# Two-layer attention and MLP kernel: Vector score tiles pick a head on an idle row tile, and the planner's settings are replaced

## The chip, the cores and the metric

The kernel runs on one core of one Trainium2 chip. The metric is device time in microseconds (us) of one execution; lower is better. The engines are TensorE (PE), VectorE (DVE), ScalarE (ACT), GpSimd (POOL) and SyncE (SP, which issues the DMAs).

## The reference

The input is x with 2048 tokens of width 512. Two rounds, each of an attention and an MLP with residuals, use the same weights. The attention has 32 heads of width 16 and no mask, so each head has a full 2048 x 2048 score matrix.

```python
def A(x, wqkv, wo):                     # H = 32, Dh = 16
    q, k, v = heads(x @ wqkv)
    p = softmax(q @ k.T * Dh ** -0.5)
    return merge(p @ v) @ wo
def B(x, w1, b1, w2, b2):               # F = 1376
    return gelu(layernorm(x) @ w1 + b1) @ w2 + b2
x = x + A(layernorm(x)); x = x + B(layernorm(x))
x = x + A(layernorm(x)); x = x + B(layernorm(x))
```

## The kernel before

**The tiling.** Layers are numbered 1 and 3 for the two attentions. Attention work is cut into segments: a chunk of queries (512 tokens; the last chunk of layer 3 is cut in two of 256) times a group of four heads. A segment has 64 score tiles of 128 keys x 512 queries (in the last two chunks one tile holds two key blocks of 256 queries), 4096 over the whole program. The four heads of a group lie on partitions 0, 32, 64 and 96, so that the score matmul of head `hp` uses the 32-row tile `hp` of TensorE's array; four such row tiles can hold four matmuls at once. The tiles of a segment are listed key block by key block, and in a block head by head.

**Two ways to the exponential.** Most score tiles go to ScalarE: `flow_scores` takes two or three tiles at a time in turn (after an opening with two at a time), puts them into PSUM banks 0 to 2 or 3 to 4, and one ACTIVATE (line 1414) writes exp of the whole group to `PT`. The tiles of every third key block (`DK` = 3, 6, 9, 12, 15) may go to VectorE instead ("d" tiles, list `todod` of the segment). Such a tile is put in bank 5 (`DLANE`) or bank 7 (`MISCB`); `d_load` (line 1512) adds a constant and writes 16-bit integers that are the bits of an approximate exp, and `job_d` (line 1545) makes three shifted copies of two tiles at a time. The four versions are multiplied with four scaled versions of the values (`V`, `vs`). A d tile that VectorE has not taken by the time the other tiles are used up goes to ScalarE.

**Values.** `try_pv` collects ready tiles and issues the value matmuls (line 1615) on the four 32-column tiles of the array, one column tile for each head, into bank 6; a d tile needs four of them, a ScalarE tile one. When a segment is complete its sums are transposed (line 1645), divided and stored. The linear layers (lines 941, 1694, 1749, 1792) run on the full array beside all this. [...]

**The order.** No engine's order is written by hand. At build time a planner (`Sched`) keeps a clock for each engine with a cost for each operation, always starts the task that can start first, and fixes the five instruction orders. They run on the chip in that order, with semaphores where one engine needs another's result. After planning, `refill` puts matmuls on zeros (`zw`, lines 1321, 1323, 1325) into TensorE's planned gaps.

A d tile is chosen by `take_d`, in three places: with a group of ScalarE tiles (`flow_scores`, which passes the heads of that group), after a VectorE task or a load of a d tile when VectorE has little to do (`d_solo`), and in a long gap of TensorE (`fill_pe`). The head is chosen by one line, and `d_solo` and `fill_pe` pass an empty list of heads:

```python
        j = next((j for j in sg["todod"] if sg["tiles"][j][1] not in hps), sg["todod"][0])
```

**The settings.** `Hint` holds six settings of the planner: how little work VectorE must have for `d_solo` (`D_IDLE`), how full a group of value matmuls must be (`PV_LEAST`), how long other TensorE work may delay the next scores (`HOLD_LATE`), how near in time a ready tile must be (`PV_NEAR`), the priority of the second half of a linear matmul (`LIN2`), and whether a tile of a ScalarE group may be given to VectorE (`D_STEAL`). There are ten modes: the base, and nine that change one setting. Every 8 groups `flow_scores` calls `HINT.at`, which reads the next mode from the string `ORDER`.

Of the kernel before, what the change touches and what calls it, by code (L numbers as in the profile page):

```python
# [506 lines left out]

class Hint:
    BASE = dict(D_IDLE=1.2, PV_LEAST=0.75, HOLD_LATE=0.4, PV_NEAR=0.7, LIN2=9, D_STEAL=0)
    MODES = ({}, dict(D_IDLE=0.8), dict(D_IDLE=1.7), dict(PV_LEAST=0.6), dict(PV_LEAST=0.9), dict(HOLD_LATE=0.2), dict(HOLD_LATE=0.6), dict(PV_NEAR=0.4), dict(LIN2=0.9), dict(D_STEAL=1.0))  # L510
    STEP = 8
    ORDER = '0550000002700000070000000900000050000000000400000000000000000000040000000050000070000000300000004000300050000090000000000070040010000000007002040000050804080004'

    def mode(self, k):
        self.__dict__.update(self.BASE)
        self.__dict__.update(self.MODES[k])

    def at(self, step):
        self.mode(int(self.ORDER[step]) if step < len(self.ORDER) else 0)


HINT = Hint()
# [3 lines left out]
class Builder:  # L526
# [806 lines left out]
    def flow_scores(self):  # L1333

        S_, P = self.S_, self.P
        self.cur = 0
        gi = 0
        self.batch = None
        self.ptuse = {}
        self.lane_busy = False  # L1340
        self.lanes = {}
        self.nsteal = 0
        self.dload = 0
        for b in range(4):
            S_.retire("mb", b, ("ret", b))
        last = {}
        while True:
            if gi % Hint.STEP == 0:
                HINT.at(gi // Hint.STEP)
            self.advance()  # L1350
            if self.cur == len(self.segs):
                break
            sg = self.segs[self.cur]
            if not self.wide and not (sg["L"] == 1 and sg["nparts"] == 2 and sg["part"] == 0):
                self.wide = True
                gi += gi % 2
                for b in (4, 5):
                    S_.retire("mb", b, ("ret", b))
            if self.wide:
                b0, G = ((0, 3), (3, 2))[gi % 2]  # L1360
            else:
                b0, G = ((0, 2), (2, 2))[gi % 2]
            grp = []
            while len(grp) < G:
                self.advance()
                if self.cur == len(self.segs):
                    break
                sg = self.segs[self.cur]
                grp.append((sg, (sg["todo"] or sg["todod"]).pop(0)))
            for sg, j in grp:  # L1370
                if sg["nt"] - self.left(sg) >= GELU_FROM * sg["nt"]:
                    S_.mark(("under", sg["i"]))
            banks = list(range(b0, b0 + len(grp)))
            keys = [("ret", b) for b in banks] + [("free", last[b]) for b in banks if b in last]
            for sg, j in grp:
                keys += [("qt", sg["i"])] + self.kv_keys(sg, sg["tiles"][j][0])
            yield ("keys", keys)
            for b in banks:
                last[b] = gi
            ptn = "pt3" if gi % 2 == 0 else "pt2"  # L1380
            self.starved = not S_.pools[ptn].free
            if self.starved:
                self.try_pv()
            pt = yield ("get", ptn)
            self.starved = False
            yield ("ready", "pe", (), [("ps", b) for b in banks])
            dts = []
            while self.wide and len(grp) + len(dts) < 4:
                d = self.take_d([s_["tiles"][j][1] for s_, j in grp] + [s_["tiles"][j][1] for s_, j, b, bt, w in dts])
                if d is None:  # L1390
                    break
                dts.append(d)
            if self.wide and not dts and len(grp) in (3,) and self.dve_work() < HINT.D_STEAL:
                d = self.take_d([s_["tiles"][j][1] for s_, j in grp[:-1]], banks[-1])
                if d is not None:
                    sg, j = grp.pop()
                    (sg["todod"] if set(sg["tiles"][j][0]) <= set(DK) else sg["todo"]).insert(0, j)
                    last[banks.pop()] = ("lane", gi)
                    self.lanes[d[2]] = ("lane", gi)
                    self.cur = min(self.cur, sg["i"])  # L1400
                    self.nsteal += 1
                    dts.append(d)
            ops = []
            for (sg, j), b in zip(grp, banks):
                ops.append(self.score(sg, j, b))
            for d in dts:
                S_.submit(Task("pe", -0.5, self.score(d[0], d[1], d[2])), cb=lambda d=d: self.d_load(d))
            if len(ops[0]) > 1:
                ops = [[o[i] for o in ops] for i in range(len(ops[0]))]
            ops = [o for part in ops for o in part]  # L1410
            yield Task("pe", 0.0, ops)
            n = len(grp)
            self.ptuse[(ptn, pt)] = n
            S_.submit(Task("act", 1e-5 * gi, [I(lambda e, pt=pt, n=n, b0=b0: e.activation(out=self.PT[:, pt:pt + n, :], in_=self.ps[:, b0:b0 + n, :], func=ACTF.Exp, scale=EXPS),  # L1414
                                                [("ps", b) for b in banks], [("pt", pt + k) for k in range(n)], 0.19 + 0.4275 * n)]),
                      cb=lambda grp=grp, pt=pt, gi=gi, ptn=ptn: (S_.mark(("free", gi)), self.p_ready([(sg, j, ("pt", pt + k), self.PT[:, pt + k, :], (ptn, pt), 0) for k, (sg, j) in enumerate(grp)])))
            if self.batch is not None and not dts and self.cur < len(self.segs) and self.left(self.segs[self.cur]) < DTAIL and self.batch["tiles"][0][0] is self.segs[self.cur]:
                self.close_batch()
            gi += 1
        yield ("keys", [("free", g) for g in set(last.values())])  # L1420
        for b in range(6):
            S_.release("mb", b)
        S_.mark(("scores_done",))
# [19 lines left out]
    def take_d(self, hps, lane=None):  # L1443

        S_, P = self.S_, self.P
        self.advance()
        if self.cur == len(self.segs) or self.dload > 1 or P.free["dve"] - S_.now > 1.3 or sum(o[4] for t in S_.pend["dve"] for o in t.ops) > DBACK:
            return None
        if self.batch is None and (not S_.pools["dp"].free or S_.pools["dp"].waiters or self.flying >= DFLY):
            return None  # L1450
        mb = S_.pools["mb"]
        soon = lambda b: P.ready("pe", (), [("ps", b)]) <= max(S_.now, P.free["pe"]) + 0.1
        if lane is not None:
            b = lane
        elif not self.lane_busy and ("ret", DLANE) in S_.done and soon(DLANE):
            b = DLANE
        elif MISCB in mb.free and not mb.waiters and soon(MISCB):
            b = MISCB
        else:
            return None  # L1460
        sg = self.segs[self.cur]
        if self.left(sg) < DTAIL:
            if self.cur + 1 == len(self.segs):
                return None
            sg = self.segs[self.cur + 1]
            if sg["nt"] - self.left(sg) >= (DAHEAD if ("retq", 5) in S_.done else DAHEAD // 2):
                return None
        if not sg["todod"]:
            return None
        j = next((j for j in sg["todod"] if sg["tiles"][j][1] not in hps), sg["todod"][0])  # L1470
        kbs = sg["tiles"][j][0]
        if not all(k in self.S_.done for k in [("qt", sg["i"])] + self.kv_keys(sg, kbs) + [("vs", sg["i"], kb) for kb in kbs]):
            return None
        if b == DLANE:
            self.lane_busy = True
        elif lane is None:
            mb.free.remove(b)
        self.dload += 1
        sg["todod"].remove(j)
        sg["n"] += len(SHIFT) - 1  # L1480
        bt = self.batch
        if bt is None:
            bt = self.batch = {"unit": S_.pools["dp"].free.pop(0), "tiles": [], "loaded": 0, "closed": False}
            self.ptuse[("dp", bt["unit"])] = 1
            self.flying += 1
        w = len(bt["tiles"])
        bt["tiles"].append((sg, j))
        if w + 1 == DBATCH:
            self.batch = None
        return (sg, j, b, bt, w)  # L1490

    def d_solo(self):

        S_ = self.S_
        if not self.wide or self.dve_work() > HINT.D_IDLE:
            return
        d = self.take_d([])
        if d is not None:
            S_.submit(Task("pe", D_PRIO, self.score(d[0], d[1], d[2])), cb=lambda: self.d_load(d))

# [474 lines left out]
```

## Time and profile before

| what | value |
|---|---|
| median of 3 runs | 1582.37 us (1582.03 to 1583.13) |
| the profiled execution | 1583.48 us, of which the span is 1581.7 us |
| PE busy | 1549.1 us, 98% of the span |
| ACT busy | 1524.5 us, 96% |
| DVE busy | 1450.7 us, 92% |
| POOL busy | 332.3 us, 21% |
| exps on ACT (line 1414) | 1279 instructions, 1445.8 us |
| loads of d tiles on DVE (line 1512) | 946 instructions, 631.8 us |
| shifted copies on DVE (line 1545) | 1440 instructions, 558.2 us |

The table is from the page of one profiled execution. The span is the time from its first to its last instruction; the execution's own time holds 1.8 us more. Busy time is the time in which an engine ran at least one instruction, so overlapping instructions are counted once; a mean duration times a count can therefore be more than the busy time. PE's busy time contains the matmuls on zeros. In lines about groups, the part after the first bar is busy time and mean nanoseconds of one instruction, the part after the second bar is the idle time just before such instructions and what ended most of it.

### The profile page before, as it was taken

To read this page: it belongs to the slowest core of one execution; us is meant where nothing else is said; L and a number is where in the kernel's file an instruction comes from. 1 tells how busy PE (TensorE), PEld (TensorE's weight loads), DVE (VectorE), ACT (ScalarE), POOL (GpSimd) and SP (SyncE) were. 2 spreads that over 40 slices of the span, in tenths; PEclk is the share of its full clock that TensorE was granted. 3 is DMA by queue.
4 is the path that set the end of the run, shared out by engine and by line. 5 is a ranking of instruction groups with operands and counts; after the bars stand their busy time and mean duration, and the time that the engine had idled before them with its cause. 6 is when DMAs were issued, how large, how long until landed. Compare 5 with 4: busy or idle time off the path is not lost.

```text
span 1581.7 us, 38782 instructions
## 1 busy us (share of the span) xinstructions
PE 1549.1 (98%) x16223; PEld 471.7 (30%) x16223; DVE 1450.7 (92%) x3210; ACT 1524.5 (96%) x1362; POOL 332.3 (21%) x574
## 2 busy tenths in 40 slices
PE   9999999999999999999999999999999999999998
PEld 3222222222222222222222223222222222344454
DVE  7689999999999899989999898999999999999894
ACT  6999999999999999999999999999999999999996
POOL 5586321001210022202212227320001000020100
PEclk9999999999999999999999999999999999999999
DMA  6663112103321133213742223210001100221200
GB/s 173 114 143 88 32 31 44 48 24 70 85 45 47 28 75 76 55 38 99 133 62 56 61 71 76 54 33 22 24 22 38 32 23 18 40 41 35 50 19 21
DMA packets 212463, 88.77 MB, mean 56 GB/s; under 512 B 183835, under 2 KB 206656, under 8 KB 212288
## 3 DMA queue, kind: packets, MB, share of 16 engines
q1 hardware_dynamic: 212288, 86.29, 24.4%
q8 instruction: 127, 2.08, 0.6%
q14 instruction: 48, 0.39, 0.1%
HBM read 34.65 MB, written 19.48 MB: 34 GB/s over the span
## 4 chain that ended last, share of the span: by engine, by line
PE 54%; DVE 23%; ACT 20%; issue 2%; POOL 0%; SPq 0%; DMA 0%; POOLq 0%; DVEq 0%
ACT PT L1414 19%; PE ps L1429 19%; PE ps L1615 16%; DVE dp L1512 10%; DVE dp L1545 7%; PE ps L1749 5%; PE ps L1792 4%; PE ps L941 4%; PE ps L1321 3%; PE ps L1694 1%; DVE accT L1645 1%; PE ps L1325 1%; PE ps L1323 1%; ACT h L1784 1%; DVE n L1006 1%
## 5 line engine op out<-in xcount | busy, mean ns | idle before, releaser
L1414 ACT ACTIVATE PT<-ps 128x1536 bf16<-128x1536 f32 (+1 forms) x1279 | 1445.8, 1259 | 30.2 <-PE ps L1429 24.2
L1512 DVE TENSOR_SCALAR dp<-ps 128x512 uint16<-128x512 f32 x946 | 631.8, 679 | 60.4 <-PE ps L1429 57.9
L1429 PE MATMUL ps<-QT,KT 32*128 32x512 bf16 (+1 forms) x4608 | 672.3, 358 | 13.9 <-DVE dp L1512 5.2
L1545 DVE TENSOR_SCALAR dp<-dp 128x1024 uint16<-128x1024 uint16 x1440 | 558.2, 427 | 6.1 <-PE ps L1615 1.7
L1615 PE MATMUL ps<-PT,V 128*17 128x512 bf16 (+1 forms) x3540 | 468.9, 358 | 0.1
L1615 PE MATMUL ps<-dp,vs 128*17 128x512 bf16 (+1 forms) x3204 | 438.5, 357 | 0.9 <-DVE dp L1545 0.9
L1429 PEld LDWEIGHTS ps<-QT,KT 32*128 32x128 bf16 x4608 | 172.1, 91 | 546.6 <-ACT PT L1414 258.5
L1158 POOL TENSOR_SCALAR QT<-qraw,scl,qbias 128x512 bf16<-128x512 bf16 (+1 forms) x84 | 71.6, 853 | 807.6 <-PE ps L1429 803.2
L1615 PE MATMUL ps<-dp,V 128*17 128x512 bf16 (+1 forms) x1068 | 212.5, 357 | 2.7 <-DVE accT L1645 2.1
L1323 PE MATMUL ps<-zw 32*128 32x444 bf16 (+4 forms) x697 | 189.2, 322 | 0.0
L1615 PEld LDWEIGHTS ps<-dp,vs 128*17 128x17 bf16 x3204 | 111.4, 88 | 118.8 <-issue 97.0
L1615 PEld LDWEIGHTS ps<-PT,V 128*17 128x17 bf16 x3540 | 112.9, 88 | 112.6 <-issue 99.4
L1321 PE MATMUL ps<-zw 128*128 128x448 bf16 (+13 forms) x475 | 113.7, 335 | 2.9 <-DVE ps L741 1.7
L1325 PE MATMUL ps<-zw 128*32 128x448 bf16 (+24 forms) x1202 | 111.7, 320 | 0.3 <-DVE dp L1512 0.2
L1749 PE MATMUL ps<-yT,wf 128*128 128x512 bf16 (+3 forms) x396 | 101.7, 360 | 1.6 <-DVE accT L1645 0.8
L941 PE MATMUL ps<-wqkv,xnT 128*128 128x512 bf16 x336 | 95.3, 383 | 1.6 <-DVE qy L1013 0.4
L1183 POOL TENSOR_SCALAR vs<-V 128x340 bf16<-128x340 bf16 (+2 forms) x72 | 60.5, 842 | 30.3 <-PE ps L1615 23.1
L1615 PEld LDWEIGHTS ps<-dp,V 128*17 128x17 bf16 x1068 | 52.4, 88 | 43.9 <-issue 23.1
L1645 DVE STREAM_TRANSPOSE accT<-ps 128x512 f32<-128x512 f32 (+1 forms) x88 | 57.7, 656 | 8.0 <-PE ps L1615 6.7
L1773 DVE TENSOR_SCALAR h<-ps,b1c 128x512 bf16<-128x512 f32 (+2 forms) x88 | 62.0, 705 | 3.2 <-PE ps L1749 2.9
L1321 PEld LDWEIGHTS ps<-zw 128*128 128x128 bf16 x475 | 37.2, 99 | 72.7 <-issue 44.0
L882 POOL TENSOR_SCALAR xn<-xres,rs,nmr 128x512 bf16<-128x512 bf16 x54 | 53.4, 996 | 10.6 <-DMA xnT<-xn 5.1
(179 smaller groups left out, 888.4 us busy)
## 6 DMA issues: line engine op xcount, KB each, us to landing
vs<-vs_scr SPq DMA_DIRECT2D x56, 255.0 KB, 2.7
wf<-in_B_w_dram SPq DMA_DIRECT2D x90, 128.0 KB, 2.5
q_scr<-qk SPq DMA_DIRECT2D x22, 256.0 KB, 2.1
k_scr<-qk SPq DMA_DIRECT2D x12, 256.0 KB, 2.0
out_dram<-xres SPq DMA_DIRECT2D x16, 128.0 KB, 1.7
vs_scr<-vs SPq DMA_DIRECT2D x8, 255.0 KB, 3.5
xres<-in_A_x_dram SPq DMA_DIRECT2D x7, 256.0 KB, 3.2
v_scr<-vst SPq DMA_DIRECT2D x12, 136.0 KB, 2.0
```

Of the source, the lines that this page charges most:

```text
L941: yield Task("pe", prio if c0 == 0 else min(prio, HINT.LIN2), [I(lambda e, c=c: e.matmul(self.ps[:, b, :], lhsT=xnT[:, c, :], rhs=self.wqk ...
L1158: yield Task(eng, 0.4, [I(lambda e: e.tensor_scalar(out=self.QT[:, q, 0:W], in0=src, scalar1=self.scl[:, k, hg:hg + 1], scalar2=self.qbias ...
L1321: fn = lambda e: e.matmul(self.ps[:, b, 0:w], lhsT=self.zw[:, 0:128], rhs=self.zw[:, 0:w], start=st, stop=st, skip_group_check=True)
L1323: fn = lambda e: e.matmul(self.ps[:, b, 0:w], lhsT=self.zw[32 * p:32 * p + 32, 0:128], rhs=self.zw[32 * p:32 * p + 32, 0:w], start=st, sto ...
L1325: fn = lambda e: e.matmul(self.ps[32 * p:32 * p + 32, b, 0:w], lhsT=self.zw[:, 0:32], rhs=self.zw[:, 0:w], start=st, stop=st, skip_group_c ...
L1414: S_.submit(Task("act", 1e-5 * gi, [I(lambda e, pt=pt, n=n, b0=b0: e.activation(out=self.PT[:, pt:pt + n, :], in_=self.ps[:, b0:b0 + n, :] ...
L1429: return [I(lambda e, kb=kb, i=i: e.matmul(self.ps[:, b, i * W:(i + 1) * W], lhsT=self.KT[32 * hp:32 * hp + 32, hg, kb * 128:(kb + 1) * 12 ...
L1512: self.S_.submit(Task("dve", 0.0, [I(lambda e: e.tensor_scalar(out=self.dp[:, u, w * 512:(w + 1) * 512], in0=self.ps[:, b, :], scalar1=BIT ...
L1545: yield Task("dve", pr, [I(lambda e, k=k, v=v: e.tensor_scalar(out=self.dp[:, v, 0:N], in0=self.dp[:, u, 0:N], scalar1=float(SHIFT[k]), sc ...
L1615: ops.append((nth[j, sh] + 0.1 * i, I(lambda e, hp=hp, v=v, ap=ap[:, i * W:(i + 1) * W], first=first and i == 0, W=W: e.matmul(self.ps[32 ...
L1645: yield Task("dve", 0.3, [I(lambda e: e.transpose(self.accT[:, a, 0:W], self.ps[:, ACCB, 0:W]), [("ps", ACCB)], [RA], 0.17 + 0.535 * W / 5 ...
L1749: yield Task("pe", pr if c0 == 0 else min(pr, HINT.LIN2), [I(lambda e, c=c: e.matmul(self.ps[0:M, b, off:off + W], lhsT=self.w1(fc, c), rh ...
```

## The change

Three things are changed.

1. `take_d` looks at TensorE before it picks the head of a d tile. It works out the time `t` at which the tile could start, collects the heads whose row tile is still busy then (only if TensorE is in row mode), and picks the first d tile whose head is not busy; among those, one whose head is not in the list `hps` it was given.
2. `flow_scores` remembers the heads of the group that it is about to issue in `self.group` until the group has been issued, and `d_solo` passes this list where it passed an empty one.
3. The string `ORDER` is new: 159 digits where there were 160, with 104 that are not the base mode where there were 27. The first digits differ as well, from the second on. The ten modes are the same; digits are read in base 36, which makes no difference for 0 to 9.

```diff
-    ORDER = '0550000002700000070000000900000050000000000400000000000000000000040000000050000070000000300000004000300050000090000000000070040010000000007002040000050804080004'
+    ORDER = '005555003180310019413073040330407885455803010030028129180000730440110100040007002434339950550723032320234308400953830012333075908409591072300003698000049440985'
...
     def at(self, step):
-        self.mode(int(self.ORDER[step]) if step < len(self.ORDER) else 0)
+        self.mode(int(self.ORDER[step], 36) if step < len(self.ORDER) else 0)
...
         self.batch = None
+        self.group = []
         self.ptuse = {}
...
+            self.group = [s_["tiles"][j][1] for s_, j in grp]
             yield ("keys", keys)
...
             yield Task("pe", 0.0, ops)
+            self.group = []
             n = len(grp)
...
-        j = next((j for j in sg["todod"] if sg["tiles"][j][1] not in hps), sg["todod"][0])
+        t = max(P.free["pe"], S_.now, P.ready("pe", (), [("ps", b)]))
+        busy = [hp for hp, x in P.tiles.items() if x > t + 0.02] if P.tiling == "row" else []
+        j = min(sg["todod"], key=lambda j: (sg["tiles"][j][1] in busy, sg["tiles"][j][1] in hps))
...
-        d = self.take_d([])
+        d = self.take_d(self.group)
```

`P.tiles` is the planner's record of when each row tile becomes free, and `P.free["pe"]` of when TensorE can issue again. As the planner makes the whole order anew, instructions move on every engine.

More of the change, by code (lines that the diff above doesn't have):

```diff
@@ L509 @@
     BASE = dict(D_IDLE=1.2, PV_LEAST=0.75, HOLD_LATE=0.4, PV_NEAR=0.7, LIN2=9, D_STEAL=0)
-    MODES = ({}, dict(D_IDLE=0.8), dict(D_IDLE=1.7), dict(PV_LEAST=0.6), dict(PV_LEAST=0.9), dict(HOLD_LATE=0.2), dict(HOLD_LATE=0.6), dict(PV_NEAR=0.4), dict(LIN2=0.9), dict(D_STEAL=1.0))
+    MODES = (dict(), dict(D_IDLE=0.8), dict(D_IDLE=1.7), dict(PV_LEAST=0.6), dict(PV_LEAST=0.9), dict(HOLD_LATE=0.2), dict(HOLD_LATE=0.6), dict(PV_NEAR=0.4), dict(LIN2=0.9), dict(D_STEAL=1.0))
     STEP = 8
-    ORDER = '0550000002700000070000000900000050000000000400000000000000000000040000000050000070000000300000004000300050000090000000000070040010000000007002040000050804080004'
+    ORDER = '005555003180310019413073040330407885455803010030028129180000730440110100040007002434339950550723032320234308400953830012333075908409591072300003698000049440985'
     def mode(self, k):
```

## The prediction

> **What bounds the kernel now.** I read the page's first part, then busy time by stretch, then what ScalarE (ACT) waits for, then the groups kept apart by shape, then stretches of the timeline. The page (engine, busy us, share, instructions):
>
> ```profile
> PE 1549.1 (98%) x16223; PEld 471.7 (30%) x16223; DVE 1450.7 (92%) x3210; ACT 1524.5 (96%) x1362; POOL 332.3 (21%) x574
> ```
>
> Three engines look full. PE's 98% holds matmuls on zeros (lines 1321, 1323, 1325), so it is not the measure. The stretches (columns: busy us of PE, weight load, DVE, ACT, POOL; clock; DMA) show more:
>
> ```profile
> 40.00:1560.00 1520.00, 1494.79 (x15882) 447.55 (x15885) 1414.17 (x3111) 1490.58 (x1312) 308.01 (x507) 1.00 0.24 54
> 640.00:960.00 320.00, 314.00 (x2938) 88.20 (x2930) 297.52 (x648) 305.93 (x262) 71.70 (x124) 1.00 0.35 75
> 120.00:1480.00 1360.00, 1338.14 (x13938) 389.15 (x13930) 1288.30 (x2840) 1335.49 (x1168) 251.21 (x421) 1.00 0.23 51
> ```
>
> From 40 to 1560 us ACT idles 1520 - 1490.6 = 29.4 us, 14.1 of them between 640 and 960 us, where layer 1's end meets layer 3's start. In the long middle (120 to 1480 us) DVE idles 1360 - 1288.3 = 71.7 us. So ACT is the bound; what it waits for between 40 and 1560 us, and between 640 and 960 us (us in total, times, longest):
>
> ```profile
> ACT PT L1414 <- PE ps L1429: 21.6, 61, 1.7
> ACT dw L1665 <- DVE dw L1664: 1.3, 4, 0.4
> ```
> ```profile
> ACT PT L1414 <- PE ps L1429: 12.6, 23, 1.7
> ```
>
> It waits for scores from PE, hardly for DVE. The groups by shape give the prices:
>
> ```profile
> L1414 ACT ACTIVATE PT<-ps 128x1536 bf16<-128x1536 f32 x593 | 882.1, 1487 | 14.9 <-PE ps L1429 9.6
> L1414 ACT ACTIVATE PT<-ps 128x1024 bf16<-128x1024 f32 x685 | 718.0, 1063 | 15.3 <-PE ps L1429 14.6
> L1512 DVE TENSOR_SCALAR dp<-ps 128x512 uint16<-128x512 f32 x946 | 631.8, 679 | 60.4 <-PE ps L1429 57.9
> L1545 DVE TENSOR_SCALAR dp<-dp 128x1024 uint16<-128x1024 uint16 x1398 | 548.4, 431 | 6.1 <-PE ps L1615 1.7
> L1545 DVE TENSOR_SCALAR dp<-dp 128x512 uint16<-128x512 uint16 x42 | 11.0, 293 | 0.1
> ```
>
> One 512-column score tile costs ACT 1487 - 1063 = 424 ns. Exps overlap, so the instruction's own cost comes from the page's 1445.8 us for all 1279 of them: (1445.8 - 3150 x 0.424) / 1279 = 0.086 us, with 4096 - 946 = 3150 tiles on ACT. A stretch without a wait agrees within 1%: 34 exps in 38.69 us against 34 x (2.5 x 0.424 + 0.086) = 39.0.
>
> ```profile
> 1126.65 38.69 ACT L1414 ACTIVATE PT<-ps 128x1536 bf16<-128x1536 f32 x34
> ```
>
> The timeline of PE tells what a row tile is worth (start, length from the first start to the last end):
>
> ```profile
> 1153.49 0.60 PE L1429 MATMUL ps<-QT,KT 32*128 32x512 bf16 x4
> 1154.03 0.60 PE L1792 MATMUL ps<-wqkv,h 128*128 128x512 bf16 x2
> 1154.56 0.39 PE L1429 MATMUL ps<-QT,KT 32*128 32x512 bf16 x2
> 1154.88 0.60 PE L1792 MATMUL ps<-wqkv,h 128*128 128x512 bf16 x2
> ```
> ```profile
> 25.19 0.40 PE L1429 MATMUL ps<-QT,KT 32*128 32x512 bf16 x4
> 25.52 1.25 PE L1321 MATMUL ps<-zw 128*128 128x448 bf16 x6
> ```
>
> Four scores on four heads hold PE 25.52 - 25.19 = 0.33 us; four of which two share a head hold it 0.54. Two scores side by side: 0.32. So a matmul behind another on one row tile costs 0.21 us, one on an idle row tile nothing, and 0.32 - 0.21 = 0.11 us goes with the change of tiling mode.
>
> **What the Trainium skill says.** "TensorEngine Tiling (Array Packing)", Key Properties: a change of tiling mode drains TensorE, and tiles work in parallel. The trace agrees, with 0.11 us for the change and 0.33 against 0.54 for four scores. "ScalarE: Activation LUTs", What ACT_TABLE_LOAD costs: 186 ns + 0.833 ns per column, and some 93 ns of overlap back to back. That is 427 ns a tile and 93 ns an instruction; the trace has 424 and 86, which I use. "TensorE: Matmul & The Clock Gate", part 1: the array's clock falls after too little work in a window of about 3.4 us. The clock column above is 1.00 throughout; no fall shows.
>
> **The change, part by part.** The planner is in the kernel, so built instruction orders can be compared; all counts below are from there.
>
> *ACT.* Vector tiles rise from 946 to 964, so ACT's fall from 3150 to 3132, in 1271 instructions instead of 1279 (three fewer of 1536 columns, four of 1024, the one of 512). 18 x 0.424 + 8 x 0.086 = **8.3 us** less. All of it lies on the bounding engine. The gelus and their tables stay, as do the first 100 or so ACT instructions, and so the opening.
>
> *PE, scores.* Without the zero matmuls, I cut PE's stream into runs of one tiling mode and took in each run the fullest tile. Over all score runs that is 380.6 us at 2400 columns a us, and 313.8 after: **66.8 us** less. Runs two scores deep fall from 509 to 231, one deep rise from 562 to 885. This is what choosing the head does.
>
> *PE, given back.* The value matmuls' fullest tiles rise from 402.6 to 418.8 us (+16.2): 63 more matmuls for 18 more shifted tiles (3 x 21), and heads less even. Mode changes 2431 to 2458: 27 x 0.11 = +3.0. Net PE need: 1045.0 + 267 = 1312 before; 994.4 + 270 = 1265 after, **47.6 us** less. It is not time gained; it is worth what it takes from ACT's 21.6 us of waits.
>
> *How much of those.* I cut both orders into 40 parts of equal score work and set PE's need (0.115 us a change) against ACT's (tiles x 0.459). Leaving out the first and last parts, PE needs more than ACT in seven parts before, by 25.3 us in all, near the 21.6 measured. After, it does in three, by 8.2: at the join of the layers 11.7 becomes 7.3, elsewhere 13.6 becomes 0.9. Taken whole, two thirds of the waits would go, 15 us. But 12.6 of the waits lie at the join, where the relief is 38% (4.7 us). Of the 9.0 elsewhere, 3.4 come before 120 us, where little changes, and the rest are waits of mostly 0.2 to 0.4 us, about the length of a score run, which less work need not remove: I count a quarter (1.4). So I take **6 us**; ends: 15 gained, and 6 lost if the dense new order waits in other places.
>
> *DVE.* 18 loads x 0.668 (631.8/946) = 12.0; 39 more shifts of 1024 x 0.392 = 15.3; 24 fewer of 512 x 0.26 = -6.3: 21 us more. It is covered by the 71.7 us of idle in the middle, which shrinks to about 42 as the stretch shortens by 8. Costed at nothing; if the cover is gone it shows as PE waiting for banks 5 and 7.
>
> *Zero matmuls.* 2374 to 2838: 759 more on column tiles, 244 fewer on row tiles, 51 fewer full. They stand in PE's planned gaps. Work weighted by tile size, zeros included, goes from 1005 to 1021 us, so the clock has no reason to fall. Cost: nothing; bounds 0 to +3 us if they hold up scores.
>
> *POOL and SP.* 578 and 524 instructions in both, some rearranged: query transposes (1144) and loads of vs (1174) pass the xnT transposes (918). POOL waits 803 us on PE for QT, that is, it works far ahead; these moves cost nothing while that lead holds. For DMA I find at most 2 us waits in the trace: bounds -1 to +2.
>
> Sum against the profiled execution: span 1581.7 - 8.3 - 6 = 1567.4; that execution took 1583.48 (1.8 around the span), so 1569.2. The median of the runs shown is 1582.37, 1.1 below it: **1568 us**.
>
> **The rivals.**
> *PE was the whole limit of the waits.* Two thirds or more of ACT's waits vanish, as the cut in 40 parts says word for word: 1582.4 - 8.3 - 15 = 1559, and down to 1554. For it: PE holds 54% of the chain that ended last. Against: the join of the layers keeps its dense linear work. Chance 0.15.
> *The relief goes nowhere.* Freed PE time is filled with zeros and ACT's waits stay or grow by up to 6: 1574 to 1580. For it: the trace has ACT 98% busy in the middle already, so there is little to win. Chance 0.20, a fifth of it within 0.2%.
> *DVE becomes the bound: slower.* With about 42 us of slack in 1350, a late load (1512) keeps bank 5 or 7; PE runs in order, so the next score of a Vector tile waits, the ACT scores behind it wait, and ACT idles. PE already waits 58.4 us for 1512 in 154 places. It decides from the point where new ACT idle passes 8.3 us; if ACT's waits double with it (+22), 1582.4 - 8.3 + 22 = 1596. Against: of all these waits just 21.6 us reach ACT now. Chance 0.08.
> *It doesn't do what it says.* Excluded for the order (depth falls), not for the chip: four row tiles could run slower than two. The 0.33 us for four speaks against it; it would end within 0.2% (0.02).
>
> **How the numbers follow.** Forecast (1562 to 1574): 0.55; rivals 0.15, 0.20, 0.08, 0.02. A measurement of this kernel tells about 0.2% (3.2 us) from no change. Faster: 0.55 + 0.15 + 0.16 = 0.86; same: 0.04 + 0.02 = 0.06; slower 0.08. The range 1556 to 1579 holds the forecast, most of the first rival and most of the second.
>
> **What would show it.** ACT busy near 1516; 964 loads at 0.68; score groups in runs of 0.39 rather than 0.60; less DVE idle before 1512; ACT's waits on PE under 21.6, the fall outside 640 to 960 us larger. Wrong if ACT's idle between 40 us and its last exp grows past 37 us, if waits name DVE, or if the clock column drops.

## The result and the profile after

The changed kernel takes 1565.56 us (median; 1563.94 to 1566.4 in 4 runs), the kernel before 1582.75 us in the runs beside it. The ratio is 0.9887 (95% interval 0.987 to 0.9904), so it is 17.2 us faster; 14.4 were predicted. Its profiled execution took 1565.7 us with a span of 1563.9 us. The mean granted clock was 0.999 in all four runs; of the 39 runs of the kernel before that stand beside e11, those at 0.999 took 1.9 us longer (median) than those at 1.000. Lines behind the added ones stand up to 5 lower: 1414 is now 1417, 1429 is 1432, 1512 is 1517, 1545 is 1550, 1615 is 1620.

The page's first part:

```profile
PE 1519.7 (97%) x16750; PEld 486.1 (31%) x16750; DVE 1458.7 (93%) x3243; ACT 1510.3 (97%) x1354; POOL 328.9 (21%) x574
```

The span is 17.8 us shorter and ACT is busy 14.2 us less. The busy time of the engines by stretch (the ends moved with the span), and what ACT waits for from 40 us to its last exp, then between 640 and 960 us:

```profile
40.00:1545.00 1505.00, 1468.35 (x16446) 463.26 (x16439) 1424.81 (x3153) 1478.47 (x1306) 304.56 (x508) 1.00 0.25 54
640.00:960.00 320.00, 310.74 (x3060) 91.86 (x3062) 297.76 (x648) 309.19 (x267) 76.40 (x134) 1.00 0.36 75
120.00:1470.00 1350.00, 1317.17 (x14530) 406.35 (x14534) 1299.16 (x2876) 1331.84 (x1169) 244.14 (x416) 1.00 0.23 51
```
```profile
ACT PT L1417 <- PE ps L1432: 19.7, 39, 3.4
```
```profile
ACT PT L1417 <- PE ps L1432: 9.2, 13, 2.4
```

The waits are 39 instead of 61, but their sum falls by only 1.9 us, and only at the join of the layers (12.6 to 9.2). DVE's idle in the middle falls from 71.7 to 50.8 us. The groups by shape:

```profile
L1417 ACT ACTIVATE PT<-ps 128x1536 bf16<-128x1536 f32 x590 | 890.5, 1509 | 14.9 <-PE ps L1432 12.2
L1417 ACT ACTIVATE PT<-ps 128x1024 bf16<-128x1024 f32 x681 | 726.9, 1081 | 10.8 <-PE ps L1432 10.2
L1517 DVE TENSOR_SCALAR dp<-ps 128x512 uint16<-128x512 f32 x964 | 641.8, 679 | 27.1 <-PE ps L1432 24.1
L1550 DVE TENSOR_SCALAR dp<-dp 128x1024 uint16<-128x1024 uint16 x1437 | 561.2, 430 | 4.4 <-PE ps L1620 2.2
L1550 DVE TENSOR_SCALAR dp<-dp 128x512 uint16<-128x512 uint16 x18 | 4.6, 286 | 0.0
```

An exp's mean duration rose by 20 ns, and yet ACT is busy for less. An instruction that waits in ACT's queue behind a running exp starts before that one ends, and the overlap is counted in both. A longer mean here means more exps that were ready in time: of those with 1536 columns, 377 had all their scores 0.2 us or more before the running exp ended, and 441 have after the change. With less lead the recorded duration is 1.45 us, with more it is up to 1.53 us (medians), at the same time from end to end. DVE's idle before a load of a d tile (line 1517) halved, from 60.4 to 27.1 us.

All score matmuls, before and after:

```profile
L1429 PE MATMUL ps<-QT,KT 32*128 32x512 bf16 (+1 forms) x4608 | 672.3, 358 | 13.9 <-DVE dp L1512 5.2
```
```profile
L1432 PE MATMUL ps<-QT,KT 32*128 32x512 bf16 (+1 forms) x4608 | 600.8, 359 | 22.0 <-ACT PT L1417 9.1
```

The same 4608 matmuls keep PE busy for 71.5 us less. Four scores in a row, whose length says that each has its own row tile:

```profile
1119.77 0.39 PE L1432 MATMUL ps<-QT,KT 32*128 32x512 bf16 x4
1120.09 0.38 PE L1620 MATMUL ps<-dp,vs 128*17 128x512 bf16 x1
```

Four scores hold PE for 1120.09 - 1119.77 = 0.32 us, much as four on different heads did in the opening of the kernel before (0.33). And the longest pieces of the chain that ended last (start, us, what), first before, then after:

```profile
1145.14 53.24 ACT PT L1414 x47
```
```profile
1118.08 99.54 ACT PT L1417 x88
1299.73 96.50 ACT PT L1417 x85
```

In that chain ACT now runs up to 88 exps in a row without anything holding it up, where it was 47. Of the whole chain ACT now holds 44% and PE 31%; before, PE held 54% and ACT 20%.

**Where the 17 us come from.** Waits miss a part of what a late exp costs, so I took the time from the end of one exp to the end of the next. Where the second was queued well ahead, the median is 1.343 us for 1536 columns and 0.916 for 1024, in both kernels: 0.427 us a tile and 0.062 an instruction. (The Trainium skill has 0.833 ns a column in "ScalarE: Activation LUTs", What ACT_TABLE_LOAD costs, an estimated 427 ns for 512 columns; the trace agrees with it better than with the 424 ns that I had.) What is above that price I call late time. A late exp costs its idle time and also the overlap of 0.1 us or more that it loses. The profiled executions then split into the exps at that price, late time, the rest from the first exp to the last (gelus, tables, small exps), and the tail after the last exp, all in us; the opening before the first exp (24 to 26 us) is left out:

```
kernel               exps   late (exps late)  rest  tail
before             1424.3   45.8  (174)       64.8  21.0
after              1416.2   35.1  (115)       63.7  23.2
e1 head only       1426.5   65.3  (211)       64.8  21.1
e2 order only      1423.6   65.0  (197)       64.5  21.8
e3 new, base       1421.9   65.3  (213)       64.6  21.6
e4 old, base       1423.8   62.2  (198)       63.2  22.5
e5 shuffled        1425.2   69.5  (190)       64.6  26.3
e8 half            1420.1   51.1  (148)       64.7  21.6
e9 none beside     1416.2   34.1  (113)       63.2  21.5
e10 DVE more       1416.2   52.9  (162)       65.0  21.2
e11 score twice    1416.2   59.6  (217)       63.5  23.2
e12 no zero        1416.2   67.9  (167)       64.6  23.7
e13 old, searched  1424.2   45.8  (136)       64.3  21.1
e14 new, searched  1415.7   44.7  (158)       63.7  20.8
```

The change: exps -8.1, late time -10.7, rest -1.1, tail +2.2. The tail holds the last MLP, and grew because TensorE ran at half clock for 3.4 us of it, which a mean of 0.999 hides. A stretch of it (clock in the third column from the end) and its first 12 matmuls, in the changed kernel and then in e9, where the same instructions meet no half clock:

```profile
1550.00:1555.00 5.00, 5.00 (x26) 2.95 (x24) 0.00 (x0) 2.14 (x6) 0.00 (x0) 0.68 0.00 0
1549.05 2.06 PE L1754 MATMUL ps<-yT,wf 128*128 128x256 bf16 x12 [0.52 <-DVE yT L1880]
```
```profile
1550.00:1555.00 5.00, 5.00 (x37) 3.42 (x35) 0.00 (x0) 2.69 (x6) 0.00 (x0) 1.00 0.00 0
1547.47 1.48 PE L1754 MATMUL ps<-yT,wf 128*128 128x256 bf16 x12 [0.52 <-DVE yT L1880]
```

What brings the first two terms is the question of the experiments.

### The profile page after: what moved, and what is told of

The parts are those of the page before. It is cut to its first block, busy times and chain, and to the rows that moved or that the text cites. A ratio compares the mean times of both kernels' runs of the same rounds, so it can differ in the third digit from the quotient of the medians.

```text
span 1563.9 us, 39887 instructions
## 1 busy us (share of the span) xinstructions
PE 1519.7 (97%) x16750; PEld 486.1 (31%) x16750; DVE 1458.7 (93%) x3243; ACT 1510.3 (97%) x1354; POOL 328.9 (21%) x574
## 4 chain that ended last, share of the span: by engine, by line
ACT 44%; PE 31%; DVE 21%; issue 1%; POOL 1%; DMA 1%; SPq 0%; POOLq 0%; DVEq 0%
ACT PT L1417 42%; PE ps L1432 10%; PE ps L1620 8%; DVE dp L1517 8%; DVE dp L1550 6%; PE ps L1797 4%; PE ps L941 3%; PE ps L1754 3%; PE ps L1321 2%; ACT h L1789 1%; DVE n L1006 1%; DVE accT L1650 1%; PE ps L1699 1%; PE ps L1325 1%; DVE sq L982 1%
## 5 line engine op out<-in xcount | busy, mean ns | idle before, releaser
L1517 DVE TENSOR_SCALAR dp<-ps 128x512 uint16<-128x512 f32 x964 | 641.8, 679 | 27.1 <-PE ps L1432 24.1
L1432 PE MATMUL ps<-QT,KT 32*128 32x512 bf16 (+1 forms) x4608 | 600.8, 359 | 22.0 <-ACT PT L1417 9.1
L1550 DVE TENSOR_SCALAR dp<-dp 128x1024 uint16<-128x1024 uint16 (+1 forms) x1455 | 564.7, 428 | 4.4 <-PE ps L1620 2.2
L1620 PE MATMUL ps<-PT,V 128*17 128x512 bf16 (+1 forms) x3519 | 490.2, 358 | 0.2 <-ACT PT L1417 0.2
L1620 PE MATMUL ps<-dp,vs 128*17 128x512 bf16 (+1 forms) x3267 | 472.6, 357 | 1.1 <-DVE dp L1550 1.0
L1158 POOL TENSOR_SCALAR QT<-qraw,scl,qbias 128x512 bf16<-128x512 bf16 (+1 forms) x84 | 71.5, 851 | 772.7 <-PE ps L1432 770.0
L1620 PE MATMUL ps<-dp,V 128*17 128x512 bf16 (+1 forms) x1089 | 224.1, 357 | 1.7 <-DVE accT L1650 1.4
L1325 PE MATMUL ps<-zw 128*32 128x448 bf16 (+23 forms) x1961 | 192.0, 324 | 0.2
L1323 PE MATMUL ps<-zw 32*128 32x444 bf16 (+2 forms) x453 | 128.3, 316 | 0.0
L1321 PE MATMUL ps<-zw 128*128 128x448 bf16 (+14 forms) x424 | 102.2, 338 | 4.1 <-DVE ps L741 1.7
L1325 PEld LDWEIGHTS ps<-zw 128*32 128x32 bf16 x1961 | 67.9, 95 | 25.0 <-DVE dp L1517 4.3
L1620 PEld LDWEIGHTS ps<-dp,V 128*17 128x17 bf16 x1089 | 54.7, 88 | 37.7 <-issue 19.7
L1778 DVE TENSOR_SCALAR h<-ps,b1c 128x512 bf16<-128x512 f32 (+2 forms) x88 | 61.9, 703 | 1.1 <-PE ps L1754 0.8
```

The source lines that it names most:

```text
L1158: yield Task(eng, 0.4, [I(lambda e: e.tensor_scalar(out=self.QT[:, q, 0:W], in0=src, scalar1=self.scl[:, k, hg:hg + 1], scalar2=self.qbias ...
L1321: fn = lambda e: e.matmul(self.ps[:, b, 0:w], lhsT=self.zw[:, 0:128], rhs=self.zw[:, 0:w], start=st, stop=st, skip_group_check=True)
L1323: fn = lambda e: e.matmul(self.ps[:, b, 0:w], lhsT=self.zw[32 * p:32 * p + 32, 0:128], rhs=self.zw[32 * p:32 * p + 32, 0:w], start=st, sto ...
L1325: fn = lambda e: e.matmul(self.ps[32 * p:32 * p + 32, b, 0:w], lhsT=self.zw[:, 0:32], rhs=self.zw[:, 0:w], start=st, stop=st, skip_group_c ...
L1432: return [I(lambda e, kb=kb, i=i: e.matmul(self.ps[:, b, i * W:(i + 1) * W], lhsT=self.KT[32 * hp:32 * hp + 32, hg, kb * 128:(kb + 1) * 12 ...
L1517: self.S_.submit(Task("dve", 0.0, [I(lambda e: e.tensor_scalar(out=self.dp[:, u, w * 512:(w + 1) * 512], in0=self.ps[:, b, :], scalar1=BIT ...
```

## The experiments

Each kernel was timed beside the kernel before; ratios are to that.

**e1 to e5: one half of the change at a time.** e1 is the changed kernel with the old string, e2 the old kernel with the new string:

```diff
-    ORDER = '005555003180310019413073...'     # e1
+    ORDER = '0550000002700000070000000900...'
```

> The new head choice with the old ORDER. In its built order VectorE takes 941 tiles (946 before, 964 after), so ScalarE's exps should cost 5 x 0.427 + 1 x 0.062 = 2.2 us more than before; the fullest row tiles fall from 380.6 to 328.1 us, three quarters of the change's fall. Theory A (ScalarE sets the time: tiles taken off it plus exps that start late): 2 us up for the tiles, 3 to 8 us down for fewer late exps, so 1577 to 1582 us. Rival B (the freed row tiles alone bring the gain): three quarters of 17 us, so about 1570 us. Rival C (the settings alone bring it): no change, 1582 to 1586 us.

Measured: 1604.09 us, ratio 1.0126 (1.0109 to 1.0143). All three were wrong. Three quarters of the fall in row depth (the fullest row tiles, summed over the score runs) are there, and the kernel is slower by 20 us; late time rose to 65.3 us.

> The old head choice with the new ORDER. Built order: 948 Vector tiles, row tiles 384.5 us, TensorE's need 1330 us against 1312 before and 1265 after. Theory A: 0.7 us off for the tiles, but TensorE has more to do, so late exps stay or grow: 1580 to 1592 us. Rival B: no gain or slower, 1582 to 1590 us. Rival C: most of the gain, 1566 to 1572 us.

Measured: 1602.94 us, ratio 1.012 (1.01 to 1.014), worse than any of the three. C falls in this form: the new string is no better string as such.

e3 has an empty string, so base mode throughout; e5 has the new digits shuffled from the ninth on.

> The new head choice with every setting at its base mode (an empty ORDER). Built order: 951 Vector tiles, 1274 exps, row tiles 324.3 us. Theory A: (1424.3 - 1421.9) = 2.4 us off for the tiles, and some of the late exps gone: 1573 to 1581 us. Rival B: about 1569 us. Rival C: 1582 us or more, as nothing was searched.

Measured: 1599.52 us, ratio 1.0098 (1.0081 to 1.0115).

> The new head choice with the new ORDER's digits in a random order from the ninth on, so as many steps leave the base mode, but not where the search put them. Built order: 944 Vector tiles, 1279 exps, row tiles 328.8 us, 2502 mode changes. Theory A: 0.9 us more exps than before, fewer late ones by the row tiles: 1577 to 1586 us. If it is the density of the modes that brings the gain rather than their places: 1566 to 1570 us.

Measured: 1612.09 us, ratio 1.0175 (1.0158 to 1.0192). The slowest of all: in this one shuffle, digits away from their places do harm. So this string fits one head choice and one sequence of steps, and neither half of the change alone brings any of the gain.

**e4: does freed TensorE time help by itself?** The old kernel with an empty string, to stand beside e3.

> The old head choice with every setting at its base mode. Against e3 (new head choice, base, 1599.5 us) it tells what the head choice brings when neither order was searched for. Built order: 947 Vector tiles (951 in e3), row tiles 379.8 us (324.3), TensorE's need 1312 us (1273). Theory D (the freed row tiles are worth something by themselves): 2 us for the tiles and 8 to 15 us of late exps, so 1607 to 1616 us. Theory E (late exps follow from how the order's pieces meet, not from TensorE's total need): within 4 us of e3, 1597 to 1603 us.

Measured: 1599.01 us, ratio 1.0096 (1.0079 to 1.0113), 0.5 us from e3. Within theory E's range: 55 us less row depth and four more Vector tiles came to nothing at base mode. (The tiles took 1.9 us off the exps, and late time grew by 3.1.) That TensorE's total need does not set the late time is shown here; what does, theory E leaves vague. ACT's waits, e3 first, then e4:

```profile
ACT PT L1417 <- PE ps L1432: 40.5, 102, 4.7
```
```profile
ACT PT L1414 <- PE ps L1429: 38.6, 78, 3.7
```

The waits are alike although TensorE's need differs by 40 us.

**e8: do the digits act where they stand?**

```diff
-    ORDER = '0055550031803100194130...'   # 159 digits
+    ORDER = '0055550031803100194130...'   # the first 80 of them
```

> The changed kernel with only the first 80 digits of ORDER, the base mode from there on. Built order: 955 Vector tiles, 1273 exps, row tiles 317.7 us. If the digits act where they stand (each removes late exps in its own stretch): the first half of the program as in the changed kernel, the second as in e3, so about (1565.6 + 1599.5) / 2 = 1582 us, and ScalarE's waits for scores up to 800 us as few as in the changed kernel. If the string acts only as a whole: near 1599 us.

Measured: 1584.1 us, ratio 0.9998 (0.999 to 1.0007), against 1582 expected. ACT's waits from 40 to 790 us and after, for e8, then the same for the changed kernel:

```profile
ACT PT L1417 <- PE ps L1432: 11.5, 23, 3.4
ACT PT L1417 <- PE ps L1432: 19.5, 40, 4.5
```
```profile
ACT PT L1417 <- PE ps L1432: 11.6, 23, 3.4
ACT PT L1417 <- PE ps L1432: 8.0, 16, 2.4
```

The first halves had to agree, since the planner makes the same order up to the 80th digit. The news is the second half, which has 11.5 us more of waits: a good first half does not carry over, and the digits act in the half in which they stand. Single digits were not tried.

**e13 and e14: both head choices with a search of their own.** What e1 to e5 leave open is whether the old head choice would have done as well with a string made for it. So I searched a string for each choice with the same program and effort: digit by digit, keeping the five best strings, judged by how far the planner has come 12 steps later.

```diff
-    ORDER = '0550000002700000070000000900...'
+    ORDER = '0050608020040230000745403004...'   # e13, old head choice
...
+    ORDER = '0050000090725510100007005841...'   # e14, new head choice
```

> The old head choice with an ORDER of 160 digits searched for it in the same way as for e14 (step by step, five best strings kept, each judged by how far the planner has come 12 steps later; no digit of the change's ORDER is used). Built order: 946 Vector tiles, 1277 exps, row tiles 380.4 us, all as before; TensorE's need 1312 us. If a fresh search is all that the change needed (rival C): near the changed kernel, 1564 to 1569 us. If the head choice is needed as well: ScalarE's exps stay at 1424.2 us (1416.2 in the changed kernel), fewer late ones, 1572 to 1580 us.

Measured: 1580.39 us, ratio 0.9977 (0.9969 to 0.9985).

> The new head choice with an ORDER searched for it in exactly the same way and with the same effort as in e13. Built order: 965 Vector tiles, 1271 exps (1415.7 us), row tiles 315.5 us. If the head choice is worth something once each choice has settings searched for it: 8.5 us for the tiles and some late exps below e13, so 1564 to 1571 us. If not: within 3 us of e13.

Measured: 1571.79 us, ratio 0.9919 (0.9902 to 0.9935). The two differ by 8.6 us. The table says in what: the exps, 1424.2 against 1415.7, while late time is 45.8 and 44.7 (in profiled executions 2.6 and 0.6 us above their medians). So this is what the head choice was worth, in one search for each: with it the search found room for 19 more Vector tiles; with the old choice it found none (946). By what steps the freed row tiles make that room was not tested. The string of the change then has 10 us less late time than that of e14, and the two kernels differ in nothing else: that part is the quality of the string. A still better search for the old choice was not tried.

**What the planner's own clock says.** Neither the prediction nor the expectations used it. At the end of planning, zero matmuls included, it stands at 1581.3 us in the kernel before and 1557.0 in the changed one; at 1598.1, 1600.2, 1595.6, 1594.3 and 1606.5 in e1 to e5, 1578.3 in e8, 1571.6 in e13 and 1563.4 in e14. Each measured median lies 1 to 9 us above its own, in nearly the same order. So the late time that e1 to e5 did not foresee is in the planned order already and could have been read there. The changed kernel, e13 and e14 lie furthest above theirs, by 8 to 9 us: not all that a string gains on this clock arrives.

**e9 and e12: the zero matmuls.** The planned order is that of the changed kernel in both. e9 leaves out those beside other matmuls, e12 all that `refill` places.

```diff
-                if op.spec[6] and not any(o.t0 < op.t0 + 0.05 ...
+                if False and op.spec[6] and not any(o.t0 < op.t0 + 0.05 ...
...
-            if op.eng == "pe":                 # e12 as well
-                fill(op)
```

> The changed kernel with the same planned order, but without the zero matmuls that refill puts beside score and value matmuls (1802 zero matmuls instead of 2838). If they cost nothing and only keep the clock: either the same time (1564 to 1567 us, clock 1.00) or, if they are needed, a lower clock and a longer time by the share lost. If they hold up scores (bound of the prediction: 3 us): up to 3 us faster, 1562 us.

Measured: 1562.06 us (1561.31 to 1562.78), ratio 0.9861 (0.9846 to 0.9876). It is the fastest kernel of the study, 3.5 us under the changed one. The two were not run in one set and their intervals meet at the edges, but no run of one reaches the other's. Of the 3.2 us between the profiled spans, late time explains 1.0, the rest 0.5 and the tail 1.7, and the tail's part is the half clock: all four runs of the changed kernel have a mean clock of 0.999, all four of e9 1.000. So in delayed work these zero matmuls cost 1 to 1.5 us; whether they also bring about the half clock in the tail, or only move the time at which it falls, is open.

> The changed kernel with the same planned order and no zero matmul at all during the planned program (0 instead of 2838; the real work weighted by tile size is 860 us of the span, 55%). If the clock needs them: a clock below 1.00 in places, longer matmuls, and a time above 1566 us, perhaps by tens of us. If they only stand in the way: 1555 to 1562 us, as without those beside other matmuls it was 1562.1.

Measured: 1593.72 us (median of 19 runs, 1585.55 to 1600.66), ratio 1.0055 (1.0039 to 1.007). A twentieth took 2799.25 us at clock 1.0, which nothing here explains. Its whole span in the profiled execution (1600.49 us; the clock again third from the end):

```profile
0.00:1599.00 1599.00, 1421.76 (x13791) 416.08 (x13912) 1464.58 (x3243) 1516.03 (x1354) 328.93 (x574) 0.96 0.25 55
```

The mean clock falls to 0.96, and late time nearly doubles. This is the clock gate of the Trainium skill ("TensorE: Matmul & The Clock Gate", part 1: half clock after an idle window of about 3.4 us), and the trace agrees: 23 stretches at half clock, each 3.4 us long or a whole multiple of that, 126 us in all. The profiled execution before the change shows none. In these runs the zero matmuls in the gaps are needed, and those beside other work are not.

**e10 and e11: what slack is left once the order is fixed?** Both keep every instruction of the changed kernel in its place and add work that the planner counts as zero. e10 adds 71 copies on VectorE, e11 issues every third Vector tile's score twice.

```diff
+    I(lambda e: e.tensor_copy(out=self.junk[:, 0:W], in_=self.accT[:, a, 0:W]), [RA], [("junk",)], 0.0, (), 0.0)   # e10
...
+    rep = 2 if b in (DLANE, MISCB) and self.nsc % 3 == 0 else 1                     # e11, in score()
```

> The changed kernel with the same planned order and 71 extra copies on VectorE of 512 columns (one at the end of nearly every segment, results unused), which the planner counts as zero, so that no instruction moves. At 0.3 to 0.6 us each this is 21 to 43 us of VectorE work. If VectorE has the cover that the prediction names (about 42 us of idle in the middle): up to 5 us slower, as most of it is absorbed. If VectorE sets the time too (the rival on the slower side): most of the added work appears, 15 to 40 us slower, and ScalarE's waits grow.

Measured: 1581.82 us, ratio 0.9982 (0.9975 to 0.9989). What PE and ACT wait for in the changed kernel:

```profile
PEld ps L1432 <- DVE dp L1517: 69.0, 183, 0.9
...
ACT PT L1417 <- PE ps L1432: 22.3, 40, 3.4
```

And in e10, after the copies themselves:

```profile
L1687 DVE CAST junk<-accT 128x512 bf16<-128x512 f32 (+1 forms) x71 | 27.9, 393 | 0.0
```
```profile
PEld ps L1433 <- DVE dp L1518: 87.8, 221, 1.3
...
ACT PT L1418 <- PE ps L1433: 34.6, 73, 3.4
```

The copies last 27.9 us as recorded, and raise VectorE's busy time by 21.0 us, as they overlap their neighbours. They cost 16.3 us over the changed kernel (15.0 by the ratios), so 58% of the one and 78% of the other; late time rises by 17.8 us. PE waits longer for loads of d tiles, and the scores behind these come late, so ACT's waits rise as well.

> The changed kernel with the same planned order, but every third Vector tile's score matmul is issued twice into the same bank, uncounted by the planner. The fullest row tiles rise from 313.8 to 375.7 us, about where they were before the change (380.6), while the tiles of each engine and their order stay. If the depth of the score runs is worth something once the order is fixed (theory D): most of the 10.7 us of late exps come back and more, 1574 to 1590 us. If TensorE has the room (theory E): under 5 us slower, 1565 to 1570 us.

Measured: 1587.93 us, ratio 1.0019 (1.0011 to 1.0027). 61.9 us of row depth cost 22.4 us (20.9 by the ratios), 36%, and late time rises by 24.5 us. Theory D holds here and fell in e4. The two agree if, in a fixed order, a score run that takes longer than planned delays what follows, while a shorter run gains only as much as the planner then puts in its place. That is a reading of the two runs; no run tests it by itself.

## Why the prediction was right, and where its reasons were not

**ACT's exps**: predicted 8.3 us less by 18 tiles and 8 instructions, measured 8.1 at the back-to-back price. This step was right, and e13 against e14 (8.5) shows it once more. Its prices were a little off in opposite ways: 0.424 us a tile for 0.427, and 0.086 us an instruction for 0.062, since the busy time it came from also holds the overlap that late exps lose.

**The waits**: 6 us predicted, late time fell by 10.7. Two things failed. The term was sized in idle time (21.6 us), which fell by 1.9 only; the overlap lost by 174 late exps, 59 more than after, was not in it. And the step that cut both orders into 40 parts and set PE's need against ACT's was the wrong cause. Its near match with the measured waits was chance. The same cut of the other built orders gives 22 us for e1, 16 for e3 and 25 for e4, where exps wait for 40.5, 40.5 and 38.6 us, and 32 for e13 and 15 for e14, where they wait for 30.9 and 26.6; for the kernel before it gives 26, with 24.2 us of waits. Nor does TensorE's total need follow late time: e1 has 65 us of it with a need of 1281 us instead of 1312. Late exps are a property of the planned order as a whole, which the head choice and the string make together. That the sum of the prediction came within 3 us is in part luck: a term sized at 6 for a wrong reason measured 10.7, and the tail gave 2.2 back. That the fall would be larger outside 640 to 960 us was wrong as well: there it went from 12.6 to 9.2, elsewhere from 9.0 to 10.5.

**DVE at nothing**: in its own groups, 16.5 us were added (10.0 in loads, 6.5 in shifts) where I had 21; its busy time rose by 8.0. The cover that I named is no cover: of the unplanned copies 58% of their length came through (e10). What kept the added tiles free is, as far as e10 shows, that the planner had placed them. The rival with DVE as the bound had its mechanism right (banks, PE in order, ACT behind it), as e10's waits show: 28 us of copies that the plan did not hold brought 1581.8.

**Zero matmuls at nothing, bound 3 us**: those beside other matmuls cost 1 to 1.5 us in delayed work, inside the bound. That the clock had no reason to fall was wrong in one place: it fell to half for 3.4 us in the tail, one of the prediction's own signs of being wrong, and worth the tail's 2 us or so.

**Heads on four row tiles**: 0.32 us for four scores, as priced, and 71.5 us less of busy time in scores where the count gave 66.8. **PE as the whole limit** (1559): e3 and e4 speak against it, as 55 us less row depth brought nothing there. **The relief goes nowhere**: in idle time it nearly came true (21.6 to 19.7 us), but late time fell all the same. **Same and slower**: not what happened; but the ground was thin, since the new head choice with the old string, with none or with a shuffled one (e1, e3, e5) is 16 to 28 us slower than the kernel before.

## What to carry to other kernels

Where a planner fixes the order at build time, a better local rule and the settings are one design: a rule must be judged with settings searched anew for it and for its rival, for here the settings of one did harm with the other. Look first at where the planner's own clock ends: here it told the order of nearly all the kernels. Count the work of the bounding engine in the built order, at its back-to-back price; here that term came within 0.2 us. Idle time of another engine was no cover for work that the plan didn't hold.

## What the runs showed of the hardware

A late ACTIVATE cost more than ACT's idle time: in the kernel before, 26.9 us of idle stand before exps that follow another exp, and late time is 45.8 us. The rest is overlap of about 0.1 us each that a queued exp has and a late one has not. The medians from end to end for 1536 columns in that kernel show the steps (the ends of score matmuls are modelled in a trace): 1.343 us when the last score was there 0.2 us or more before the running exp ended, 1.389 us with less lead, and 1.576 us when the score came after that.

The TensorE clock was halved for 3.4 us in the tail of the changed kernel. It held at 1.00 with 1036 zero matmuls fewer (e9) and fell to a mean of 0.96 when all 2838 were gone (e12); nothing between was tried.
